# Moving the top-k mask to GpSimd and building the attention weights from transposed scores

## The chip, the cores and the metric

The kernel runs on one core of a Trainium2 chip. The metric is the device time of one execution in microseconds. The core's engines run beside each other: TensorE (matrix products and transposes; PE in the profile, with PEld for its weight loads), VectorE (DVE), ScalarE (ACT), GpSimd (POOL), and SyncE (SP), which issues transfers here. Products land in PSUM, everything else is held in SBUF.

## The reference, cut to what matters

Attention with a top-32 mask in each row of scores, for 8 batches of 8 heads, 576 rows and 64 columns a head, then a mixture of experts over the 4608 tokens with a capacity of 80 per expert. The change concerns the first part alone.

```python
def _attn_ref(q, k, v):                       # (8, 8, 576, 64) each
    top_k = 32
    scale = 1.0 / np.sqrt(D)
    scores = scale * np.matmul(q, k.transpose(0, 1, 3, 2))
    kth = np.partition(scores, -top_k, axis=-1)[..., -top_k:-top_k + 1]
    mask = scores >= kth
    scores = np.where(mask, scores, -1000000000.0)
    scores = scores - np.max(scores, axis=-1, keepdims=True)
    attn = np.exp(scores)
    attn = attn / (np.sum(attn, axis=-1, keepdims=True) + 1e-09)
    return np.matmul(attn, v).astype(np.float32)

# then: x = attention output as (4608, 512); top-1 expert by x @ w_gate;
# each expert keeps its 80 tokens of largest gate weight;
# out = gate * relu(x @ w1[e]) @ w2[e] for those, 0 for the rest
```

## The kernel before

The work goes by head pairs: `n` counts 32 of them (8 batches, 4 pairs of heads). Each pair has four full blocks of 128 query rows and a tail block of 64. A full block gives two *units* (one per head), the tail one unit with both heads' 64 rows stacked in the 128 partitions. So there are 9 units a pair and 288 in all. One *step* of the schedule handles one unit on VectorE, while other engines are at earlier or later units.

Scores are made once for the search (`front`) and scaled by a tiny power of two when ScalarE copies them out:

```python
TINY = 2.0 ** -48
minus = ...                      # identity in bf16, times -1.0 / TINY

def front(self, n, t):           # t: row block, 0 to 4
    ps = self.four()             # the one score buffer "sp": four PSUM banks, shared
    for j in range(2):
        for h in range(2):
            ...
            nc.tensor.matmul(o, lhsT=qT[d, ...], rhs=kT[d, ...], start=True, stop=True)
    s = self.rows.tile([P, 2 * S], F32, name="s", ...)
    nc.scalar.activation(s[...], ps[...], Act.Copy, scale=TINY)
```

VectorE finds the threshold of each row: the best 8 of six sixths, the best 24 of those 48, a count of how many scores lie above the 24th, and the 24th to 32nd from the rest. Then it makes the mask:

```python
def parts(self, i):              # "G", six times a unit
    nc.vector.max(out=cand[:, j, :], in_=s[:, j * S // NG : (j + 1) * S // NG])     # L202

def search(self, i):             # letters a b c d e, then y, g, h, m
    # a, c, e: best 8 of cand (L213); b, d: those taken out (L221);
    # with e: ScalarE writes y = sign(w9[7] - s) and counts (L218)
    nc.vector.tensor_tensor(out=y, in0=s, in1=y, op=Alu.mult)                      # y, L223
    nc.vector.max(out=w9[:, 8:], in_=y)                                            # g, L225
    nc.vector.scalar_tensor_tensor(out=pick, ..., accum_out=self.thr[:, i:i+1])    # h, L228
    self.drop(i)                                                                   # m

def drop(self, i):                                                                 # L250
    self.mask[i] = self.rows.tile([P, S], BF16, name="mask", ...)
    nc.vector.tensor_scalar(self.mask[i], s, self.thr[:, i : i + 1], top[:, 0, 0:1],
                            op0=Alu.is_lt, op1=Alu.add)   # (s < threshold) + row maximum
```

The weights are needed with the keys in the partitions, so `turn_w` makes the scores a second time, transposed. The mask, transposed by a product with `minus`, is added first in the same PSUM sum. It brings both the masking and the subtraction of the row maximum; ScalarE then takes the exponential:

```python
def turn_w(self, n, t):
    for h in range(2):
        for c in range(NK):      # five groups of keys
            nc.tensor.matmul(dst[h][c], lhsT=masks[h][:, keys[c]], rhs=eye[h],
                             start=c in (0, NF), stop=False, ...)                  # L268
    for c in range(NK):
        for h in range(2):
            nc.tensor.matmul(dst[h][c], lhsT=kT[heads[h], keys[c]], rhs=qT[heads[h], rows],
                             start=False, stop=True, ...)                          # L272
    nc.scalar.activation(wT[...], ab[...], Act.Exp, scale=scale)                   # L275
    nc.scalar.activation(wT[:, 2 * NF, :m], cc[:, :m], Act.Exp, scale=scale)       # L276

def back(self, n, t):            # weights times (v, ones): sums and unnormalised output, L290
    ...
def norm(self, n, ...):          # z = 1 / sum (z, L301, L304); xn = xu * z on GpSimd (L307);
    ...                          # xn to DRAM; later its transposes through "sp" (L165), the copy
                                 # xT (L320), and the gate product lp (L325), 128 columns at a time
def turn(self, n):               # the pair's q and k transposed through "sp" (L165), copies qT, kT (L176)
    ...
```

One step issues, in this order (a letter's number is how many units it lags behind):

```python
back = dict(a=0, b=1, c=1, d=1, e=1, y=2, g=2, h=3, m=3)
for c in "GbGcGdGehGmyGga": ...
turn_w(unit i - 3)               # if it closes a row block
front(unit i + 2) or turn(next pair)
back(unit i - 4)
norm's next part
```

Of the kernel before, what the change touches and what calls it, by code (L numbers as in the profile page):

```python
# [19 lines left out]
LOW = -3.0e38  # L20
TINY = 2.0 ** -48
# [3 lines left out]
def kernel(  # L25
# [11 lines left out]
    nc = tc.nc  # L37
# [31 lines left out]
    zero = const.tile([P, Dm], F32, name="zero")  # L69
# [19 lines left out]
    nc.scalar.mul(minus, ident, -1.0 / TINY)  # L89
# [16 lines left out]
    def clear():  # L106

        r = 4 * P
        return [lambda i=i: nc.sync.dma_start(
            out[i : i + r, :].rearrange("(p r) d -> p r d", p=P),  # L110
            zero.unsqueeze(1).to_broadcast([P, r // P, Dm])) for i in range(0, N, r)]

    class Attention:


        def __init__(self, stack, lean):
            self.lean = lean
            pool = lambda name, bufs, **kw: stack.enter_context(tc.tile_pool(name=name, bufs=bufs, **kw))
            self.nat, self.qkp, self.rows = pool("nat", 1), pool("qkp", 2), pool("rows", 2)
            self.small, vpool = pool("small", 4), pool("vpool", 1)  # L120
            self.ps_s, self.ps_w, self.ps_c = (pool(n, k, space=PSUM) for n, k in (("ps_s", 1), ("ps_w", 1), ("ps_c", 2)))
            self.qk, self.turned, self.lg = {}, {}, {}
            self.s, self.top, self.low, self.cnt, self.y, self.mask, self.w, self.xu = ({} for _ in range(8))

            self.thr = vpool.tile([P, HP * UPP if lean else NU], F32, name="thr")

            self.vb = []
            for j in range(1 if lean else 3):
                t = vpool.tile([P, NF, 2, D + 1], F32, name=f"vb{j}")
                r = vpool.tile([P, 2, D + 1], F32, name=f"vr{j}")  # L130
                nc.gpsimd.memset(t[:, :, :, D : D + 1], 1.0)
                nc.gpsimd.memset(r, 0.0)
                for h in range(2):
                    nc.gpsimd.memset(r[TL * h : TL * h + TL, h, D : D + 1], 1.0)
                self.vb.append((t, r))

            self.xT = vpool.tile([P, NK * P], F32, name="xT")
            nc.gpsimd.memset(self.xT[:, S:], 0.0)

        def load(self, n, b, hp):  # L140
            one = bass.ds(b, 1)
            tiles = []
            for name, src in (("qn", q), ("kn", k)):
                t = self.nat.tile([P, NK, 2, D], F32, name=name, tag=name)
                for h in range(2):
                    nc.sync.dma_start(
                        t[:, 0:NF, h, :],
                        src[one, 2 * hp + h, : NF * P, :].rearrange("o (c p) d -> p (o c) d", p=P))
                nc.sync.dma_start(
                    t[0:TL, NF, :, :], src[one, 2 * hp : 2 * hp + 2, NF * P :, :].rearrange("o h p d -> p (o h) d"))  # L150
                tiles.append(t)
            t, r = self.vb[n % len(self.vb)]
            for h in range(2):
                nc.sync.dma_start(
                    t[:, :, h, :D], v[one, 2 * hp + h, : NF * P, :].rearrange("o (c p) d -> p (o c) d", p=P))
                nc.sync.dma_start(r[TL * h : TL * h + TL, h, :D], v[one, 2 * hp + h, NF * P :, :].rearrange("o p d -> p (o d)"))
            self.qk[n] = tiles
# [10 lines left out]
        def turn(self, n):  # L168

            ts_ = []  # L170
            four = self.four()
            for j, (src, name) in enumerate(zip(self.qk.pop(n), ("qT", "kT"))):
                t = self.qkp.tile([P, S], F32, name=name, tag=name)
                ps = four[:, 2 * j : 2 * j + 2, :].rearrange("p j c -> p (j c)")
                self.turn_in(ps, src.rearrange("p c h d -> p c (h d)"))
                nc.scalar.copy(t, ps[:, :S])  # L176
                ts_.append(t)
            self.turned[n] = ts_
# [18 lines left out]
        def parts(self, i):  # L197

            s = self.s[i]
            cand = self.small.tile([P, NG, 8], F32, name="cand", tag="cand")  # L200
            for j in range(NG):
                nc.vector.max(out=cand[:, j, :], in_=s[:, j * S // NG : (j + 1) * S // NG])  # L202
                yield
            self.top[i] = cand.rearrange("p j c -> p (j c)")

        def search(self, i):
# [24 lines left out]
            self.drop(i)  # L231
            yield
# [13 lines left out]
        def drop(self, i):  # L246

            s, top = self.s.pop(i), self.top.pop(i)
            self.mask[i] = self.rows.tile([P, S], BF16, name="mask", tag="mask", bufs=3)
            nc.vector.tensor_scalar(self.mask[i], s, self.thr[:, i : i + 1], top[:, 0, 0:1], op0=Alu.is_lt, op1=Alu.add)  # L250

        def turn_w(self, n, t):

            qT, kT = self.turned[n]
            i = n * UPP + 2 * t
            m = P if t < NF else TL
            masks = [self.mask.pop(i), self.mask.pop(i + 1)] if t < NF else [self.mask.pop(i)] * 2
            eye = [minus, minus] if t < NF else [minus[:, :TL], minus[:, TL:]]
            ab = self.ps_w.tile([P, 2, NF, P], F32, name="ab", tag="ab")
            cc = self.ps_c.tile([P, 512], F32, name="cc", tag="cc")  # L260
            rows = slice(t * P, t * P + m)
            keys = [slice(c * P, min(c * P + P, S)) for c in range(NK)]
            heads = [slice(D * h, D * h + D) for h in range(2)]
            dst = [[ab[:, h, c, :m] for c in range(NF)] + [cc[heads[h], :m]] for h in range(2)]

            for h in range(2):
                for c in range(NK):
                    nc.tensor.matmul(dst[h][c], lhsT=masks[h][:, keys[c]], rhs=eye[h], start=c in (0, NF), stop=False,  # L268
                                     skip_group_check=True)
            for c in range(NK):  # L270
                for h in range(2):
                    nc.tensor.matmul(dst[h][c], lhsT=kT[heads[h], keys[c]], rhs=qT[heads[h], rows], start=False, stop=True,  # L272
                                     skip_group_check=True)
            wT = self.rows.tile([P, 2 * NF + 1, P], F32, name="wT", tag="wT")
            nc.scalar.activation(wT[:, : 2 * NF, :m], ab.rearrange("p h c r -> p (h c) r")[:, :, :m], Act.Exp, scale=scale)  # L275
            nc.scalar.activation(wT[:, 2 * NF, :m], cc[:, :m], Act.Exp, scale=scale)  # L276
            self.w[n, t] = wT, cc

        def back(self, n, t):
# [4 lines left out]
            vb, vr = self.vb[n % len(self.vb)]  # L284
            m = P if t < NF else TL
            for h in range(2):
                o = slice(P + h * (D + 1), P + (h + 1) * (D + 1))
                for c in range(NK):
                    for r in range(0, m, TL):
                        nc.tensor.matmul(cc[r : r + TL, o], lhsT=wT[:, h * NF + c if c < NF else 2 * NF, r : r + TL],  # L290
                                         rhs=vb[:, c, h, :] if c < NF else vr[:, h, :], start=(c == 0), stop=(c == NF))
            nc.scalar.copy(self.xu[n][:m, t, :, :].rearrange("p h d -> p (h d)"), cc[:m, P : P + 2 * (D + 1)])  # L292

        def norm(self, n, b, hp, bi, nb):
# [4 lines left out]
            z = self.small.tile([P, NK, 2], F32, name="z", tag="z")  # L299
# [15 lines left out]
            while self.fronts:  # L315
                yield
            ps = self.four()[:, :2, :].rearrange("p j c -> p (j c)")
            self.turn_in(ps, xn)
            xT = self.xT
            nc.scalar.copy(xT[:, :S], ps[:, :S])  # L320
            yield
            ps = self.ps_c.tile([P, 512], F32, name="lp", tag="cc")
            lp = ps[:, : NK * E].rearrange("p (c e) -> p c e", e=E)
            for c in range(NK):
                nc.tensor.matmul(lp[:, c, :], lhsT=xT[:, c * P : (c + 1) * P], rhs=wg[:, hp, :], start=True, stop=True)  # L325
# [5 lines left out]
            else:  # L331
                part = self.small.tile([P, NK, E], F32, name="part", tag="part", bufs=2)
# [38 lines left out]
        def run(self, slow):  # L371
# [10 lines left out]
            def step(i):  # L382
# [10 lines left out]
                back = dict(a=0, b=1, c=1, d=1, e=1, y=2, g=2, h=3, m=3)  # L393
                for c in "GbGcGdGehGmyGga":
# [3 lines left out]
                    elif c == "a":  # L398
                        if i < NU:
                            next(first[i], None)  # L400
                            second[i] = self.search(i)
                            next(second[i])
                    elif i - back[c] in second:
                        next(second[i - back[c]])
                j = i - 3
# [7 lines left out]
                j = i - 4  # L413
# [10 lines left out]
            with tc.manual_schedule():  # L424
# [6 lines left out]
                while i < NU + 4 or later:  # L431
# [4 lines left out]
        def judge(self):  # L436

            small = self.small
            least = small.tile([P, 1], F32, name="least", bufs=1)
            nc.vector.tensor_reduce(least, self.thr, axis=AX, op=Alu.min)  # L440
            ps = self.ps_c.tile([P, 512], F32, name="tp", tag="cc")
            nc.tensor.transpose(ps[:1, :P], least, ident)
# [265 lines left out]
```

## Time and profile before

| | before |
|---|---|
| device time, median of 3 | 1344.43 us (1344.4 to 1352.03) |
| span of the profiled execution | 1341.7 us |
| VectorE busy | 1127.2 us (84%) |
| TensorE busy | 1081.9 us (81%) |
| ScalarE busy | 679.1 us (51%) |
| GpSimd busy | 91.8 us (7%) |
| mean granted TensorE clock | 0.908 of full |

Busy times are unions over each engine's instructions; TensorE's are pipelined, so its share is an upper view of its work. In the lines of the profile, "L202" is a line of the kernel before. A group's line gives the engine, the operation, output<-inputs, the count, then busy time in us, mean ns of one, and the idle time of the engine just before these instructions with what ended it. A line of the waits gives the engine and line that waited, for whom, then the sum in us, how many times, and the longest.

### The profile page before, as it was taken

The page shows a single profiled execution, that of the slowest core. Times are in us where ns is not written, and L with a number is a line of the kernel's source. Part 1 is how long each engine was busy: PE and PEld are TensorE (multiplying, and loading weights), DVE is VectorE, ACT ScalarE, POOL GpSimd, SP SyncE. Part 2 cuts the span into 40 slices and gives each one's busy share as a digit, 9 for nine tenths or more (in the row PEclk, how much of TensorE's full clock was granted, in tenths as well). Part 3 has the DMA queues.
Part 4 walks back from the last instruction along what each step waited for, and adds up shares of the span by engine and source line. Part 5 has one row for each costly group of instructions (what it writes and reads, how often), then busy time and mean ns, then how long its engine had stood idle before and what let it go on. Part 6 is the DMA issues. An engine that isn't in the chain of part 4 may idle for free.

```text
span 1341.7 us, 38270 instructions
## 1 busy us (share of the span) xinstructions
PE 1081.9 (81%) x14862; PEld 834.7 (62%) x14862; DVE 1127.2 (84%) x5383; ACT 679.1 (51%) x1374; POOL 91.8 (7%) x213
## 2 busy tenths in 40 slices
PE   6888888888888888888888888888888888713987
PEld 3666666666666666666666666666666666603887
DVE  5999989999998999999999998999999999585001
ACT  4565555566555556565565556555555565300111
POOL 0000000000000000000000000000000000100111
PEclk9998989999889899898899989898898998855899
DMA  5033322222222122222222211111110110120660
GB/s 142 7 96 100 99 84 69 68 68 69 68 68 56 49 63 64 60 60 59 68 68 69 53 37 37 37 37 33 33 36 21 28 37 11 30 114 5 214 221 24
DMA packets 154590, 85.93 MB, mean 64 GB/s; under 512 B 118304, under 2 KB 136736, under 8 KB 154400
## 3 DMA queue, kind: packets, MB, share of 16 engines
q1 hardware_dynamic: 153376, 80.78, 21.0%
q0 software_dynamic: 1024, 2.62, 0.7%
q8 instruction: 118, 1.93, 0.6%
q14 instruction: 72, 0.59, 0.2%
HBM read 63.19 MB, written 20.19 MB: 62 GB/s over the span
## 4 chain that ended last, share of the span: by engine, by line
PE 47%; DVE 41%; ACT 8%; issue 2%; POOL 0%; DMA 0%; POOLq 0%; DVEq 0%; ACTq 0%
PE sp L190 11%; DVE cand L202 10%; PE ab L272 9%; DVE mask L250 8%; PE cc L290 7%; DVE y L223 6%; DVE w L225 6%; DVE cand L221 4%; PE ab L268 4%; ACT s L195 4%; PE yp L616 3%; PE cc L272 3%; DVE top L213 2%; PE cc L268 2%; PE sp L165 2%
## 5 line engine op out<-in xcount | busy, mean ns | idle before, releaser
L202 DVE MAX8 cand<-s 128x8 f32<-128x96 f32 x1728 | 432.0, 250 | 76.2 <-ACT s L195 76.2
L190 PE MATMUL sp<-kT,qT 64*128 64x288 f32 (+1 forms) x1280 | 233.0, 490 | 48.3 <-ACT s L195 25.7
L275 ACT ACTIVATE wT<-ab 128x1024 f32<-128x1024 f32 (+1 forms) x160 | 150.1, 938 | 236.6 <-PE ab L272 236.6
L290 PEld LDWEIGHTS cc<-vb,wT 128*64 128x64 f32 x4608 | 197.7, 153 | 62.2 <-issue 47.2
L218 ACT ACTIVATE y<-s,w 128x576 f32<-128x576 f32 x288 | 222.9, 774 | 20.2 <-DVE w L213 19.9
L290 PE MATMUL cc<-vb,wT 128*64 128x65 f32 x4608 | 227.2, 241 | 0.0
L195 ACT ACTIVATE s<-sp 128x1152 f32<-128x1152 f32 (+1 forms) x160 | 165.5, 1034 | 112.3 <-PE sp L190 108.0
L223 DVE TENSOR_TENSOR y<-s,y 128x576 f32<-128x576 f32 x288 | 216.6, 752 | 3.4 <-ACT y L218 1.4
L225 DVE MAX8 w<-y 128x8 f32<-128x576 f32 x288 | 214.0, 743 | 0.1
L268 PEld LDWEIGHTS <-mask 128*128 128x128 bf16 (+1 forms) x1600 | 106.2, 101 | 168.2 <-DVE mask L250 122.1
L268 PE MATMUL ab<-minus,mask 128*128 128x128 bf16 (+1 forms) x1280 | 120.1, 216 | 110.0 <-DVE mask L250 106.9
L272 PE MATMUL ab<-qT,kT 64*128 64x128 f32 (+1 forms) x2560 | 193.3, 293 | 0.0
L190 PEld LDWEIGHTS sp<-kT,qT 64*128 64x128 f32 (+1 forms) x1280 | 122.3, 204 | 106.1 <-ACT s L195 44.4
L272 PEld LDWEIGHTS ab<-qT,kT 64*128 64x128 f32 x2560 | 163.6, 196 | 10.0
L250 DVE TENSOR_SCALAR mask<-s,thr,top 128x576 bf16<-128x576 f32 x288 | 166.8, 579 | 1.5 <-DVE cand L202 0.6
L213 DVE MAX8 top<-cand 128x8 f32<-128x48 f32 x576 | 111.3, 193 | 0.1
L221 DVE MATCH_REPLACE8 cand<-top,cand 128x48 f32<-128x48 f32 x576 | 111.3, 193 | 0.0
L290 PE MATMUL cc<-vr,wT 128*64 128x65 f32 x1152 | 97.5, 235 | 0.0
L268 PE MATMUL cc<-minus,mask 128*64 128x128 bf16 (+1 forms) x320 | 76.3, 238 | 0.0
L292 ACT COPY xu<-cc 128x130 f32<-128x130 f32 (+1 forms) x160 | 42.2, 264 | 64.7 <-PE cc L290 64.7
L290 PEld LDWEIGHTS cc<-vr,wT 128*64 128x64 f32 x1152 | 70.4, 151 | 0.0
L272 PE MATMUL cc<-qT,kT 64*64 64x128 f32 (+1 forms) x640 | 69.6, 297 | 0.0
(165 smaller groups left out, 996.1 us busy)
## 6 DMA issues: line engine op xcount, KB each, us to landing
w<-in_moe_w_dram SPq DMA_DIRECT2D x32, 512.0 KB, 4.7
w<-in_moe_w_dram SPq DMA_DIRECT2D x8, 2048.0 KB, 12.9
out_dram<-zero SPq DMA_DIRECT2D x9, 1024.0 KB, 8.2
qn<-in_q_dram SPq DMA_DIRECT2D x64, 128.0 KB, 2.7
kn<-in_k_dram SPq DMA_DIRECT2D x64, 128.0 KB, 2.7
vb<-in_v_dram SPq DMA_DIRECT2D x64, 128.0 KB, 2.4
xd<-xn SPq DMA_DIRECT2D x32, 256.0 KB, 2.4
qn<-in_q_dram SPq DMA_DIRECT2D x32, 32.0 KB, 2.8
```

The costliest lines, as they stand in the source:

```text
L190: nc.tensor.matmul(o, lhsT=qT[d, t * P : t * P + m], rhs=kT[d, j * HS : (j + 1) * HS], start=True, stop=True)
L195: nc.scalar.activation(s[:, : g * S].rearrange("p (j c) -> p j c", c=HS), ps[:, : 2 * g, :HS], Act.Copy, scale=TINY)
L202: nc.vector.max(out=cand[:, j, :], in_=s[:, j * S // NG : (j + 1) * S // NG])
L218: nc.scalar.activation(y, s, Act.Sign, bias=w9[:, 7:8], scale=-1.0, accum_out=cnt)
L221: nc.vector.match_replace(out=cand, in_to_replace=dst, in_values=cand, imm_value=LOW)
L223: nc.vector.tensor_tensor(out=y, in0=s, in1=y, op=Alu.mult)
L225: nc.vector.max(out=w9[:, 8:], in_=y)
L250: nc.vector.tensor_scalar(self.mask[i], s, self.thr[:, i : i + 1], top[:, 0, 0:1], op0=Alu.is_lt, op1=Alu.add)
L268: nc.tensor.matmul(dst[h][c], lhsT=masks[h][:, keys[c]], rhs=eye[h], start=c in (0, NF), stop=False, skip_group_check=True)
L272: nc.tensor.matmul(dst[h][c], lhsT=kT[heads[h], keys[c]], rhs=qT[heads[h], rows], start=False, stop=True, skip_group_check=True)
L275: nc.scalar.activation(wT[:, : 2 * NF, :m], ab.rearrange("p h c r -> p (h c) r")[:, :, :m], Act.Exp, scale=scale)
L290: nc.tensor.matmul(cc[r : r + TL, o], lhsT=wT[:, h * NF + c if c < NF else 2 * NF, r : r + TL], rhs=vb[:, c, h, :] if c < NF else vr[:, h, ...
```

## The change

The mask is made on GpSimd, as a single comparison with the threshold (1 where the score is below it), and without the row maximum: the exponential is taken of unshifted scores. In `turn_w` the second score product is gone. The scores that the search already has in SBUF are transposed into PSUM, and the mask's product with `minus` (now minus the identity) is added to them: a masked score becomes about -1 where scores are scaled by 2^-48, and the exponential with scale/TINY sends it to zero. The tail block is transposed with both heads at once, so v's tail rows are laid out to match (`vb` holds all five key groups, and the last covers the last 128 keys, with zeros in v for the keys that the fourth group has already).

So that a sum of exponentials that became too small is noticed, the final test of thresholds (`judge`), which leads to a slower path, also looks at 1/sum (`z`). The schedule lags by one more unit, the order in a step is new, the transposes of xn use the small PSUM buffers instead of "sp", and q and k are both transposed before either is copied.

```diff
-            self.drop(i)
-            yield
+        def below(self, i):
+            self.top.pop(i)
+            self.mask[i] = self.rows.tile([P, S], BF16, name="mask", tag="mask", bufs=3)
+            nc.gpsimd.tensor_scalar(self.mask[i], self.s[i], self.thr[:, i : i + 1], None, op0=Alu.is_lt)
 ...
 turn_w:
-            for h in range(2):
+            for h in range(g):                      # g = 2, in the tail 1
+                sc = self.s.pop(i + h)
                 for c in range(NK):
-                    nc.tensor.matmul(dst[h][c], lhsT=masks[h][:, keys[c]], rhs=eye[h], start=c in (0, NF), stop=False,
-                                     skip_group_check=True)
-            for c in range(NK):
-                for h in range(2):
-                    nc.tensor.matmul(dst[h][c], lhsT=kT[heads[h], keys[c]], rhs=qT[heads[h], rows], start=False, stop=True,
-                                     skip_group_check=True)
+                    nc.tensor.matmul(dst[h][c], lhsT=sc[:, keys[c]], rhs=ident, start=c == 0 or (c == NF and h == 0), stop=False,
+                                     is_transpose=True, skip_group_check=True)
+            for h in range(g):
+                mk = self.mask.pop(i + h)
+                for c in range(NK):
+                    nc.tensor.matmul(dst[h][c], lhsT=mk[:, keys[c]], rhs=minus, start=False, stop=True, skip_group_check=True)
+            nc.scalar.activation(wT[...], ab[...], Act.Exp, scale=scale / TINY)
 ...
 turn: both sets of transposes, then both copies
 norm:
-            while self.fronts:
-                yield
-            ps = self.four()[:, :2, :].rearrange("p j c -> p (j c)")
-            self.turn_in(ps, xn)
+            ps, rest = (self.ps_c.tile([P, 512], F32, name="xp", tag="cc") for _ in range(2))
+            ...
-                nc.tensor.matmul(lp[:, c, :], lhsT=xT[:, c * P : (c + 1) * P], rhs=wg[:, hp, :], start=True, stop=True)
+                for r in range(0, P, TL):
+                    nc.tensor.matmul(lp[r : r + TL, c, :], lhsT=xT[:, c * P + r : c * P + r + TL], rhs=wg[:, hp, :],
+                                     start=True, stop=True)
 ...
 the step:
-                back = dict(a=0, b=1, c=1, d=1, e=1, y=2, g=2, h=3, m=3)
-                for c in "GbGcGdGehGmyGga":
+                back = dict(a=0, b=1, c=1, d=1, e=1, y=2, g=3, h=4, m=4)
+                for c in "GhmbGcGdGeGGgay":         # m is now self.below, on GpSimd
 ...
-                j = i - 3                           # turn_w
+                j = i - 4
-                j = i - 4                           # back
+                j = i - 5
 ...
 also: the zeros that clear the output are a 128x128 tile in place of 128x512; fewer buffers for two small tiles
```

## The prediction

> **What bounds the kernel now.** I read the busy shares first, then the two engines in order of time, then the waits. The page's first part and its slices:
>
> ```profile
> PE 1081.9 (81%) x14862; PEld 834.7 (62%) x14862; DVE 1127.2 (84%) x5383; ACT 679.1 (51%) x1374; POOL 91.8 (7%) x213
> ...
> PE   6888888888888888888888888888888888713987
> DVE  5999989999998999999999998999999999585001
> POOL 0000000000000000000000000000000000100111
> ```
>
> VectorE is at nine tenths in nearly every slice up to the 34th, TensorE at eight: the attention stage. The last seventh of the span (routing and experts, from about 1160 us) the change doesn't touch. Shares alone do not say which of two busy engines sets the pace, so I went to VectorE in order of time, one unit (128 query rows of one head) from one threshold to the next:
>
> ```profile
> 603.43 0.26 DVE L202 MAX8 cand<-s 128x8 f32<-128x96 f32 x1
> 603.62 0.58 DVE L250 TENSOR_SCALAR mask<-s,thr,top 128x576 bf16<-128x576 f32 x1
> 604.12 0.75 DVE L223 TENSOR_TENSOR y<-s,y 128x576 f32<-128x576 f32 x1
> 604.79 0.25 DVE L202 MAX8 cand<-s 128x8 f32<-128x96 f32 x1
> ...
> 607.07 0.26 DVE L202 MAX8 cand<-s 128x8 f32<-128x96 f32 x1
> 607.26 0.58 DVE L250 TENSOR_SCALAR mask<-s,thr,top 128x576 bf16<-128x576 f32 x1
> ```
>
> The columns are start, duration, then the instruction. There is no gap in it: the period is 607.26 - 603.62 = 3.64 us. There are 288 units, so 288 x 3.64 = 1048 us. The groups by line say where VectorE did stand still, and the waits what TensorE did meanwhile:
>
> ```profile
> L202 DVE MAX8 cand<-s 128x8 f32<-128x96 f32 x1728 | 432.0, 250 | 76.2 <-ACT s L195 76.2
> L250 DVE TENSOR_SCALAR mask<-s,thr,top 128x576 bf16<-128x576 f32 x288 | 166.8, 579 | 1.5 <-DVE cand L202 0.6
> ```
>
> ```profile
> PEld L268 <- DVE mask L250: 122.1, 91, 2.6
> ACT s L195 <- PE sp L190: 108.0, 129, 2.4
> PE ab L268 <- DVE mask L250: 106.9, 91, 2.4
> ```
>
> 1048 + 76 us of waiting for scores, and some 14 us of reciprocals and gating, make 1138 us, which is the stage: its first search instruction starts at 12.0, its last L202 at 1151.3. So VectorE is the bound. TensorE waits 107 us for masks. The 76 us are about two stops per head pair (57 in all), the longer ones near 1.9 us, where two score products for successive row blocks must pass through the one score buffer (sp) in PSUM.
>
> **What the Trainium skill says.** *GPSIMD Engine Reference*, section 4.1 Engine selection: elementwise work with two inputs is about twice as slow there as on VectorE, with one input roughly at line rate. The trace before has no wide one-input operation on that engine; its two-input product xn (128x512) takes 1043 ns and its 128x8 add 237 ns. *SBUF — State Buffer*, section Who interferes with whom: a VectorE instruction with two SBUF inputs and a GpSimd instruction that reads SBUF exclude each other for the whole instruction; one-input VectorE instructions outside the two-port modes don't. The trace before can neither show nor deny it: its y products (L223) all last 742 to 760 ns, but GpSimd is at 7%. *TensorE: Matmul & The Clock Gate*, section Part 1: the clock falls to half after a window without enough work. The trace agrees: between 20 and 1140 us the mean granted clock is 0.93, and in the stretch 626 to 630 us, after a 1.67 us wait for a mask, it is 0.50.
>
> **The change part by part.** *VectorE loses the mask.* The next instruction starts 604.12 - 603.62 = 0.50 us after it (the 579 ns overlap their neighbours). 288 x 0.50 = 144 us, all on the engine that sets the pace. The period becomes 3.14 us, and 288 x 3.14 = 904 us. Nothing else of the search changes, only its order.
>
> *GpSimd gains the mask.* 288 comparisons of 128x576, one input. Low estimate: this engine's fill of 128x640 takes 621 ns, or about 1 ns an element with its fixed part, so 237 + 568 x 0.85 = 0.72 us. High: the two-input rate from xn, (1043 - 388)/(512 - 128) = 1.7 ns an element, so 237 + 568 x 1.7 = 1.2 us. I take 0.9: 260 us in all, under a third of the stage, so the engine is not a bound. The mask is issued just after the threshold, near a step's beginning. The one wide two-input VectorE instruction, y, is now the step's last, 2.4 us after it by the row durations. So they should not meet, except where the xn product (1.4 us with its second part) stands in GpSimd's queue: once per head pair, up to 0.4 us. 32 x 0.4 = about 12 us back.
>
> *TensorE swaps score products for transposes.* From TensorE in order of time:
>
> ```profile
> 611.55 0.40 PE L268 MATMUL ab<-minus,mask 128*128 128x128 bf16 x4 [0.48 <-DVE mask L250]
> 611.87 0.24 PE L268 MATMUL cc<-minus,mask 128*64 128x128 bf16 x1
> 612.05 1.16 PE L272 MATMUL ab<-qT,kT 64*128 64x128 f32 x16
> 613.14 0.44 PE L272 MATMUL cc<-qT,kT 64*64 64x128 f32 x4
> 613.50 0.66 PE L165 MATMUL sp<-ident,xn 128*128 128x128 f32 x4
> ```
>
> The second score product takes 613.50 - 612.05 = 1.45 us (20 passes: each f32 product appears twice). Four f32 transposes last 0.66 us; less the 0.27 of the last one, 0.39/3 = 0.13 us from one to the next, so ten take 1.3 to 1.5 us. On a full row block the swap is even. The gain is elsewhere. The 64-row tail block, now with both heads in one set of rows, does five transposes and five mask products (0.7 + 0.5 = 1.2 us) for 2.04 us before (696.43 to 698.47). The gate product in halves costs about 20 x 0.03 (from L290's rate) instead of 10 x 0.11: 0.5 us less. All ten input transposes now come before their two copies, so about 1 us of waiting for the qT copy goes (27.2 us in the waits). Per head pair, full clock: before 4 x (1.0 masks + 1.45 + 1.17 scores + 1.32 weights times v) + 3.85 tail + 1.55 turn + 0.77 + 1.14 = 27.1 us; after about 25.8. VectorE's nine units take 9 x 3.14 = 28.3 us. TensorE fits, but with 9% to spare where it had 17% (27.1 of 32.8).
>
> *What is reordered.* Transposes need only scores, so they run while a mask is still being made: the 107 us wait for masks should mostly go, and with it many half-clock stretches. The xn transposes leave the score buffer (its 21.9 us wait for xT goes). Both shorten the chain that gave VectorE's 76 us of stops. I estimate 35 left, a gain of 41. One more step of pipeline adds 3 us at the end, the new test of z about 1 us.
>
> Sum: 1344.4 - 144 - 41 + 12 + 4 = 1175 us.
>
> **The rivals.** (a) VectorE stays the bound and its stops stay too: 1344.4 - 144 + 12 + 4 = 1216. For it: the single sp buffer remains, and TensorE's share rises. Against: two of its users' waits are removed. (b) TensorE becomes the bound. At 9% to spare, any half-clock stretch stops VectorE. If TensorE were productive only 80% of the time, 25.8/0.8 = 32.3 us a head pair, 32 x 32.3 = 1032 us instead of 1138: 1238. For it: the clock at half for 7 us about once per head pair before. Against: those stretches follow mask waits. (c) GpSimd is slower than estimated. Up to about 2 us nothing happens; beyond, y waits for the port and each further 0.1 us costs 29 us. A mask of 2.5 us would use up the gain and leave 1300 to 1350. Against: even the two-input rate gives 1.2 us. (d) No stops at all and no collisions: 1344.4 - 144 - 76 + 4 = 1128, the floor.
>
> **Range and chances.** Between the floor and (b), 1130 to 1245, I put eight chances in ten, the middle at 1175. Faster by over 2% means under 1317.5: only a bad case of (c), or (b) with much waiting, gets there. Faster 0.90, within 2% 0.04, slower 0.06.
>
> **What would show it.** Right: the search period 3.14 us, L202's idle time near 35 us, the mask on GpSimd at 0.7 to 1.2 us, y still about 750 ns, ten transposes in about 1.4 us, the granted clock in the stage above 0.95. Wrong: y's mean or L202's idle time grown (port or TensorE), a wait of TensorE for GpSimd's mask as large as the old one, or a mask over 2 us.

## The result and the profile after

The changed kernel takes 1174.45 us (median, 1173.9 to 1180.85) against 1345.61: a ratio of 0.873, 95% interval 0.869 to 0.877. The prediction was 1175. The sum held; four of the steps behind it did not, and the experiments below say which.

Page of the changed kernel, busy shares and slices:

```profile
PE 936.3 (80%) x13262; PEld 754.1 (64%) x13262; DVE 998.7 (85%) x5098; ACT 696.5 (59%) x1406; POOL 613.3 (52%) x496
...
PE   6888888888888888988888888888888887216997
DVE  6998998999999999899989998999899997682111
POOL 2565565665656665566656565556566666101101
```

The pattern is the old one with a shorter stage: VectorE at nine tenths, TensorE at eight. New is GpSimd at five to six tenths: its masks alone are busy for 497 us, about twice the 260 us planned.

The groups by line (the same search line is now L203, y L224, the mask L237):

```profile
L237 POOL TENSOR_SCALAR mask<-s,thr 128x576 bf16<-128x576 f32 x288 | 497.3, 1728 | 310.9 <-DVE cand L222 301.4
L203 DVE MAX8 cand<-s 128x8 f32<-128x96 f32 x1728 | 398.0, 244 | 48.1 <-ACT s L196 47.8
...
L224 DVE TENSOR_TENSOR y<-s,y 128x576 f32<-128x576 f32 x288 | 237.1, 823 | 0.0
```

The mask lasts 1728 ns, VectorE's stops for scores fell from 76 to 48 us, and y's mean rose from 752 to 823 ns. VectorE in order of time, y to y:

```profile
502.85 0.73 DVE L224 TENSOR_TENSOR y<-s,y 128x576 f32<-128x576 f32 x1
503.51 0.24 DVE L203 MAX8 cand<-s 128x8 f32<-128x96 f32 x1
...
505.97 1.08 DVE L224 TENSOR_TENSOR y<-s,y 128x576 f32<-128x576 f32 x1
```

The period is 505.97 - 502.85 = 3.12 us, as predicted (3.14). It is also the median over all 288 units. The second y lasts 1.08 us: a delayed GpSimd mask had begun at 505.70. The usual case is the xn product, in 30 of the 32 head pairs. GpSimd first, then VectorE, both in order of time:

```profile
520.46 1.72 POOL L237 TENSOR_SCALAR mask<-s,thr 128x576 bf16<-128x576 f32 x1 [1.51 <-DVE cand L222]
522.15 1.91 POOL L311 TENSOR_TENSOR xn<-xu,z 128x512 f32<-128x512 f32 x2
```

```profile
522.34 1.47 DVE L224 TENSOR_TENSOR y<-s,y 128x576 f32<-128x576 f32 x1
```

This y began 0.19 us after xn and took twice its usual 0.74 us. 288 x (0.823 - 0.739, its median) = 24 us in all. Most of it is xn: 30 x 0.73 = 22.

TensorE's waits:

```profile
PE ab L274 <- POOL mask L237: 106.8, 87, 2.3
ACT wT L276 <- PE ab L274: 104.0, 129, 3.1
```

The wait for masks is 106.8 us, where it was 106.9 for VectorE's mask. It did not go.

### The profile page after: what moved, and what is told of

Read it like the earlier page. It is cut to its first block, busy times and chain, and to the rows that moved or that the text cites. A ratio compares the mean times of both kernels' runs of the same rounds, so it can differ in the third digit from the quotient of the medians.

```text
span 1172.7 us, 35081 instructions
## 1 busy us (share of the span) xinstructions
PE 936.3 (80%) x13262; PEld 754.1 (64%) x13262; DVE 998.7 (85%) x5098; ACT 696.5 (59%) x1406; POOL 613.3 (52%) x496
## 4 chain that ended last, share of the span: by engine, by line
DVE 60%; PE 18%; ACT 7%; POOL 7%; issue 6%; DMA 0%; SPq 0%; POOLq 0%; ACTq 0%; DVEq 0%
DVE cand L203 17%; DVE y L224 13%; DVE w L226 11%; DVE cand L222 6%; POOL mask L237 6%; ACT s L196 4%; DVE top L214 4%; PE yp L629 3%; DVE pick L229 3%; PE sp L191 2%; ACT wT L276 2%; PE cc L294 2%; DVE w L214 2%; PE ab L274 2%; PE ab L269 2%
## 5 line engine op out<-in xcount | busy, mean ns | idle before, releaser
L237 POOL TENSOR_SCALAR mask<-s,thr 128x576 bf16<-128x576 f32 x288 | 497.3, 1728 | 310.9 <-DVE cand L222 301.4
L203 DVE MAX8 cand<-s 128x8 f32<-128x96 f32 x1728 | 398.0, 244 | 48.1 <-ACT s L196 47.8
L224 DVE TENSOR_TENSOR y<-s,y 128x576 f32<-128x576 f32 x288 | 237.1, 823 | 0.0
L274 PE MATMUL ab<-minus,mask 128*128 128x128 bf16 x1152 | 112.3, 226 | 106.8 <-POOL mask L237 106.8
L196 ACT ACTIVATE s<-sp 128x1152 f32<-128x1152 f32 (+1 forms) x160 | 165.4, 1034 | 32.7 <-PE sp L191 31.5
L269 PE MATMUL ab<-ident,s 128*128 128x128 f32 x1152 | 183.1, 289 | 1.1 <-ACT wT L276 1.1
L274 PEld LDWEIGHTS <-mask 128*128 128x128 bf16 x1440 | 98.3, 101 | 124.4 <-POOL mask L237 122.2
L269 PEld LDWEIGHTS ab<-ident,s 128*128 128x128 f32 x1152 | 132.9, 146 | 21.3 <-ACT wT L276 11.7
L269 PE MATMUL cc<-ident,s 128*128 128x128 f32 x288 | 80.9, 281 | 0.0
L274 PE MATMUL cc<-minus,mask 128*128 128x128 bf16 x288 | 65.1, 226 | 0.0
L229 DVE SCALAR_TENSOR_TENSOR pick<-past,cnt,w 128x9 f32<-128x9 f32 x288 | 61.0, 212 | 0.0
L311 POOL TENSOR_TENSOR xn<-xu,z 128x512 f32<-128x512 f32 x64 | 60.5, 966 | 0.1
```

Of the source, the lines that this page charges most:

```text
L196: nc.scalar.activation(s[:, : g * S].rearrange("p (j c) -> p j c", c=HS), ps[:, : 2 * g, :HS], Act.Copy, scale=TINY)
L237: nc.gpsimd.tensor_scalar(self.mask[i], self.s[i], self.thr[:, i : i + 1], None, op0=Alu.is_lt)
L269: nc.tensor.matmul(dst[h][c], lhsT=sc[:, keys[c]], rhs=ident, start=c == 0 or (c == NF and h == 0), stop=False, is_transpose=True, skip_gr ...
L274: nc.tensor.matmul(dst[h][c], lhsT=mk[:, keys[c]], rhs=minus, start=False, stop=True, skip_group_check=True)
```

## The experiments

All were timed beside the kernel before on the same chip; its medians there were 1342 to 1350 us. Executions that ran over 1.5% above the fastest of their kernel, at a lower granted clock (one of second_product, two each of old_order_first and masks_late), are left out of the medians here. "Stops" are VectorE's idle time before its first search instruction, waiting for scores.

### mask_on_vector: the comparison back on VectorE

```diff
-            nc.gpsimd.tensor_scalar(self.mask[i], self.s[i], self.thr[:, i : i + 1], None, op0=Alu.is_lt)
+            nc.vector.tensor_scalar(self.mask[i], self.s[i], self.thr[:, i : i + 1], None, op0=Alu.is_lt)
```

> The changed kernel with the one comparison back on VectorE, all else as changed. My theory (VectorE sets the pace, the gain is the 0.50 us a unit that the mask took there): 288 x 0.50 = 144 us come back, less the some 24 us that y loses to GpSimd in the changed kernel, so about 1295 us; y back at 740 ns. Rival (the gain came from TensorE, which no longer makes the second score product): 1175 to 1200.

Measured: 1302.42 us, ratio 0.965 (0.963 to 0.968). Groups by line:

```profile
L203 DVE MAX8 cand<-s 128x8 f32<-128x96 f32 x1728 | 400.8, 246 | 9.8 <-ACT s L196 9.7
...
L237 DVE TENSOR_SCALAR mask<-s,thr 128x576 bf16<-128x576 f32 x288 | 167.6, 582 | 31.5 <-DVE pick L229 0.9
```

Given the rest of the change, the move is worth 1302 - 1174 = 128 us. VectorE's busy time rises by 1136.4 - 998.7 = 138 us. It gains 38 us of stops (48 to 10) and loses 31.5 us as the mask now stands right behind the threshold it reads (0.11 us each). With a slower VectorE the stops are nearly gone: the other engines keep up with this pace.

### second_product and product_first: is it less work on TensorE, or its place?

The schedule, GpSimd mask and buffers of the changed kernel; the weights from a second score product, as before, with the mask's products first:

```diff
-    # ten transposes of s (is_transpose), then the mask's products
+    for h in range(2):
+        for c in range(NK):
+            nc.tensor.matmul(dst[h][c], lhsT=masks[h][:, keys[c]], rhs=eye[h], start=c in (0, NF), stop=False, ...)
+    for c in range(NK):
+        for h in range(2):
+            nc.tensor.matmul(dst[h][c], lhsT=kT[heads[h], keys[c]], rhs=qT[heads[h], rows], start=False, stop=True, ...)
```

> The changed kernel's schedule, GpSimd mask and buffers, but with the mask product first and then the second score product from q and k as before (tail block and v layout as before too). My theory: TensorE's work per head pair rises by less than 1 us, to some 26.6 of VectorE's 28.1, and its mask waits can no longer be filled with transposes: 1185 to 1225. Rival (TensorE's relief is the gain): 1300 or more.

Measured: 1300.34 us, ratio 0.961 (0.957 to 0.965). My theory missed by about 75 us. The stops, from its groups by line:

```profile
L205 DVE MAX8 cand<-s 128x8 f32<-128x96 f32 x1728 | 398.5, 244 | 153.8 <-ACT s L198 153.6
```

Taken alone this speaks for the rival: 154 us of stops where the transposes leave 48. But two things differ between the kernels, how much TensorE does and whether it can do it before the mask is there. So the two loops were swapped (scores first with start, the mask's products after them with stop), the amount staying as it is:

> As second_product (schedule, GpSimd mask and buffers of the changed kernel, second score product), but with the score products first and the mask's products after them in the PSUM sum. The amount of TensorE work is that of second_product, only the place of the wait for the mask differs. If the order is what counts (work that needs no mask fills the wait): 1180 to 1220 us. If the amount counts (2.44 us for masks and second product on a full block against 1.80 us for transposes and masks): 1280 to 1305.

Measured: 1168.43 us, ratio 0.869 (0.864 to 0.874), not to be told from the changed kernel, and 12 us under the range for the order. Its groups by line:

```profile
L205 DVE MAX8 cand<-s 128x8 f32<-128x96 f32 x1728 | 397.6, 244 | 33.6 <-ACT s L198 33.4
```

Only the order of two loops moved 132 us. Ahead of the mask's products the second score product costs no time that these runs show; behind them, each wait for a mask is followed by 1.46 us more (503.13 to 504.59) before the next scores (sp) can begin. From second_product, TensorE in order of time:

```profile
503.13 1.16 PE L281 MATMUL ab<-qT,kT 64*128 64x128 f32 x16
504.23 0.44 PE L281 MATMUL cc<-qT,kT 64*64 64x128 f32 x4
504.59 1.24 PE L193 MATMUL sp<-kT,qT 64*128 64x288 f32 x8
```

TensorE's waits for masks, first in second_product, then in product_first:

```profile
PE ab L277 <- POOL mask L239: 129.0, 93, 2.1
PE ab L281 <- POOL mask L239: 46.6, 60, 1.9
```

So the swap shortens the wait itself as well as what follows it, and the granted clock between 20 and 970 us rises from 0.91 to 0.97 with it; no run tells these three apart. That the change does without a second product brought no time by itself.

### before_first: the same swap in the kernel before

```diff
 turn_w of the kernel before: the loop over kT, qT first (start), the loop over masks second (stop); nothing else
```

> The kernel before, with one thing changed: in turn_w the second score product comes first and the mask's products after it. Mask on VectorE, old schedule, old buffers. VectorE's period stays 3.64 us, so only its 76 us of stops can go: if work ahead of the wait is what frees TensorE here too, L202's idle time falls to 15 to 45 us and the time to 1290 to 1325. If the stops come from the score buffer alone: 1340 to 1347.

Measured: 1289.11 us, ratio 0.960 (0.953 to 0.967). Groups by line:

```profile
L202 DVE MAX8 cand<-s 128x8 f32<-128x96 f32 x1728 | 431.9, 250 | 36.3 <-ACT s L195 36.3
```

As expected, and one microsecond beyond the range, VectorE's stops halve, and it still works on masks. A third of the change's gain (56 to 58 of 171 us) could be had by swapping two loops.

### mask_only and old_order_first: is the new schedule needed?

```diff
 kernel before, drop():
-            nc.vector.tensor_scalar(self.mask[i], s, self.thr[:, i : i + 1], top[:, 0, 0:1], op0=Alu.is_lt, op1=Alu.add)
+            nc.gpsimd.tensor_scalar(self.mask[i], s, self.thr[:, i : i + 1], None, op0=Alu.is_lt)
 old_order_first: the same, and turn_w's loops swapped as in before_first
```

> The kernel before with nothing changed but the mask: one comparison on GpSimd in place of VectorE's two operations (no row maximum is subtracted). Old order of a step, old lags. My theory: VectorE's period falls to 3.14 us, but the mask now arrives 1.7 us and more after its threshold in a schedule with no slack for it, and it is issued just ahead of y, so y and mask exclude each other: 1230 to 1300, with L202's idle time and TensorE's mask waits well above before. Rival (order and buffers matter little): about 1200. Rival (TensorE's relief is the gain): 1340 or more.

Measured: 1528.67 us, ratio 1.132 (1.129 to 1.135): slower than the kernel before, where my theory had it faster. The time lies in the second rival's range, but mask_on_vector and product_first speak against that rival. The waits did grow as the theory said, by far more than it allowed for:

```profile
DVE cand L202 <- ACT s L195: 245.4, 107, 8.9
PEld L268 <- POOL mask L250: 187.9, 89, 3.5
PE ab L268 <- POOL mask L250: 175.5, 81, 3.4
```

VectorE stops 245 us for scores, and y waits another 101 us for ScalarE's sign. The mask lasts 1995 ns on average here, against 1728: the 153 masks that start while a y runs have a median of 2.23 us, the other 135 one of 1.72.

> The kernel before with two things changed: the mask as one comparison on GpSimd, and the second score product ahead of the mask's products. Old order of a step, old lags, old buffers. Together with mask_only (1529 us) and product_first (1168 us) it tells what the new schedule is worth. If filling the wait is enough: 1170 to 1220. If the step's new order and the extra lag are needed for a mask that takes 1.72 us: 1300 to 1450.

Measured: 1365.17 us, ratio 1.017 (1.007 to 1.028). With the score products first, the old schedule (order, lags and buffers) leaves the GpSimd mask slower than VectorE's (1289); the new one makes 1168 of it. What the order of a step and the lag are worth apart was not tested.

### through_sp: the buffers of norm and turn undone

```diff
-            ps, rest = (self.ps_c.tile([P, 512], F32, name="xp", tag="cc") for _ in range(2))
+            while self.fronts:
+                yield
+            ps = self.four()[:, :2, :].rearrange("p j c -> p (j c)")   # sp again
 and in turn: q transposed, copied, then k transposed, copied
```

> The changed kernel, but xn is transposed through the score buffer sp again, when no scores are due, and q's copy stands before k's transposes again. My theory: VectorE's stops for scores go from 48 back towards 76 us: 1185 to 1205. Rival (these stops were the larger part of the gain): 1240 or more.

Measured: 1223.37 us, ratio 0.906 (0.903 to 0.908): 49 us of the gain come from these two parts, more than the 10 to 30 expected. The loss is not where I looked: L202's stops are 27.6 us, fewer than 48, but y now waits 62.8 us for ScalarE's sign (in the changed kernel: none). One such wait, ScalarE first, then VectorE:

```profile
502.48 0.64 ACT L178 COPY kT<-sp 128x576 f32<-128x576 f32 x1 [1.50 <-PE sp L169]
504.76 0.27 ACT L295 COPY xu<-cc 128x130 f32<-128x130 f32 x1 [1.64 <-PE cc L293]
504.92 0.78 ACT L218 ACTIVATE y<-s,w 128x576 f32<-128x576 f32 x1
```

```profile
505.82 0.76 DVE L223 TENSOR_TENSOR y<-s,y 128x576 f32<-128x576 f32 x1 [3.66 <-ACT y L218]
```

The sign stands on ScalarE behind k's copy, which waits for k's transposes, and behind the copy of the weights' products (xu), which waits too. TensorE has stood 0.73 us for q's copy just before, and its mean granted clock from 501 to 505 us is 0.57. In 21 of the 22 longer waits of y the same two copies come first, so in this trace the loss stands at q's copy ahead of k's transposes and not at xn. The two parts were not undone one at a time.

### half_mask and probe: the mask's size

half_mask compares only the first 288 columns and lets TensorE read those twice. It leaves out half of the comparisons, so its output is not the reference's; all other engines do the same instructions.

```diff
-            nc.gpsimd.tensor_scalar(self.mask[i], self.s[i], self.thr[:, i : i + 1], None, op0=Alu.is_lt)
+            nc.gpsimd.tensor_scalar(self.mask[i][:, : S // 2], self.s[i][:, : S // 2], self.thr[:, i : i + 1], None, op0=Alu.is_lt)
 and the mask's products read columns 0, 128, 0, 128 and 160 on
```

> The changed kernel, but GpSimd compares only the first 288 of the 576 columns and TensorE reads those twice in place of the others. It leaves out half of the mask's comparisons, so its output is not the reference's; instructions on all other engines are as many and as large as before. If the mask's 1.72 us cost time (y held up by the port, TensorE waiting for masks): y back at 740 ns, which gives 24 us, TensorE's mask wait under 40 us, and part of the 48 us of stops: 1105 to 1145. If the mask's length is hidden: 1165 to 1175.

Measured: 1102.57 us, ratio 0.821 (0.816 to 0.825). Groups by line:

```profile
L203 DVE MAX8 cand<-s 128x8 f32<-128x96 f32 x1728 | 396.6, 243 | 9.2 <-ACT s L196 9.2
L237 POOL TENSOR_SCALAR mask<-s,thr 128x288 bf16<-128x288 f32 x288 | 289.0, 1004 | 477.6 <-DVE cand L222 464.3
...
L224 DVE TENSOR_TENSOR y<-s,y 128x576 f32<-128x576 f32 x288 | 212.8, 739 | 0.0
```

So 0.72 us less in each mask is worth 72 us: 24 by y, 39 by stops, 9 not attributed. A shorter mask ends earlier, xn starts earlier, and y comes only as xn ends (0.90 us after its start). The time is just under the range; the wait for masks fell less than expected, to 60 us, and TensorE's mean clock between 20 and 900 us is 1.00 where it was 0.94. The mask's length was not hidden.

The probe is the changed kernel with 36 GpSimd instructions ahead of it, three of each form, such as:

```diff
+        for _ in range(3):
+            G.tensor_scalar(pf_[:, :W], ps_[:, :W], 0.25, None, op0=Alu.mult)
```

> The changed kernel with 36 GpSimd instructions ahead of it, three of each form, and three comparisons on VectorE, so longer by their sum; only the durations in the trace are of use. The disputed size is the mask's 1.72 us where 0.9 was estimated. If a comparison is what costs: multiplications and copies of 128x576 take under 1 us, all comparisons about 1.7 whatever the output. If the bf16 output costs: f32 outputs under 1 us. If the scalar read from memory costs: the constant form under 1 us. If every one-input tensor_scalar costs 3 ns an element: all about 1.7, half a tile about 0.9, and only plain copies shorter.

The instructions at one line of it (min/median/max ns), for the mask's form, the multiplication, the double tile, the copy and the two-input product:

```profile
L102 POOL TENSOR_SCALAR p_b<-p_s,p_t x3: 1713/1714/1736, 2.4 to 9.2; 128x576 bf16<-128x576 f32 x3
...
L108 POOL TENSOR_SCALAR p_f<-p_s x3: 1645/1652/1652, 23.4 to 28.6; 128x576 f32<-128x576 f32 x3
...
L114 POOL TENSOR_SCALAR p_b<-p_s,p_t x3: 3187/3187/3201, 30.2 to 37.8; 128x1152 bf16<-128x1152 f32 x3
...
L118 POOL COPY p_f<-p_s x3: 654/654/654, 33.4 to 41.0; 128x576 f32<-128x576 f32 x3
...
L120 POOL TENSOR_TENSOR p_f<-p_s x3: 1387/1388/1390, 42.2 to 46.2; 128x576 f32<-128x576 f32 x3
```

The last of the four explanations holds: every tensor_scalar of this size takes 1.64 to 1.72 us, whatever its operation, output type or scalar; (3187 - 1714)/576 = 2.56 ns an element, half a tile 1.00 us. A copy takes 0.65. The whole run took 1205.37 us, with the added instructions.

### lg_late, masks_late, masks_late4: taking out the waits that are left

```diff
 lg_late:
                 nc.scalar.copy(part, lp)
+                yield
                 nc.gpsimd.tensor_tensor(out=lg, in0=lg, in1=part, op=Alu.add)
```

> The changed kernel, with the small GpSimd sum of gate parts (lg) issued one step later, so that it no longer stands in GpSimd's queue waiting 74 us in all for ScalarE's copy, with masks behind it. If late masks cost time: y's mean falls from 823 towards 770 ns and the time to 1150 to 1168. If not: 1172 to 1176.

Measured: 1170.15 us, ratio 0.871 (0.865 to 0.876), between the two ranges and no difference from the changed kernel. The queue's wait for ScalarE fell from 74 to 15 us, y's mean only to 815 ns: the 22 us by xn are still there, and only the 2 to 3 us by late masks went.

```diff
 masks_late: turn_w ends after the transposes; a step later, ahead of everything else:
+                j = i - 5
+                if 0 <= j < NU and units[j][2]:
+                    self.mask_w(*units[j][:2])      # the mask's products and the exponentials
 masks_late4: the same, mask bufs 3 -> 4, v tiles 3 -> 2
```

> The changed kernel, with the transposes where they are, but the mask's products (and the exponentials) one step later, so that TensorE finds every mask ready. GpSimd's masks and their meeting with y stay. If TensorE's 107 us wait for masks is what leads to VectorE's stops (through the late next score product and the half clock): the wait goes to nearly 0, L203's idle time from 48 to about 15, clock in the stage near 1.0: 1135 to 1155 us. If the exponentials' 1.4 us now stand openly between masks and back in every second block and take the wait's place: 1165 to 1190.

> As masks_late, with four mask buffers in place of three (and two of the v tiles in place of three, to make room). If GpSimd waits for TensorE to free a mask in masks_late, this is some us faster; if not, the same within 5 us.

Measured: 1321.42 us (ratio 0.983, 0.978 to 0.988) and 1321.83 us (0.984, 0.978 to 0.990). In the second the next pair's v is loaded over a v tile before its last products have read it, so its output is not the reference's; its work is the same. A fourth mask buffer brings nothing. The waits of masks_late4:

```profile
PE cc L301 <- ACT wT L284: 160.6, 124, 3.9
ACT s L196 <- PE sp L191: 126.0, 67, 3.7
...
DVE cand L203 <- ACT s L196: 114.1, 74, 9.6
```

The wait for masks is off the list's head, and TensorE waits 161 us for exponentials instead (13 in the changed kernel). The rival was right, and it cost more than it allowed for.

## Why the prediction was right

The kernels that tell the parts apart, in us:

| mask on | schedule and buffers | mask's products first | work without mask first |
|---|---|---|---|
| VectorE | old | 1345 (before) | 1289 |
| GpSimd | old | 1529 | 1365 |
| GpSimd | new | 1300 | 1168 (1174 by transposes) |
| VectorE | new | not run | 1302 (by transposes) |

*VectorE loses the mask: right.* 0.50 us a unit was predicted, 3.64 - 3.12 = 0.52 measured, 150 us. But the table qualifies it: the move gives 128 us only with the other two parts (1302 to 1174); move and new schedule together, without the other order on TensorE, give 45 to 50 (1300 against 1345, and against 1350 beside it); with the old schedule the move loses. The pace of a step is VectorE's only if every other engine keeps up.

*GpSimd's 0.9 us: wrong.* It is 1.73, above the high estimate of 1.2. The step that failed is taking a fill (621 ns for 128x640) as the rate of one-input arithmetic. The sentence that I drew on from the Trainium skill (*GPSIMD Engine Reference*, section 4.1 Engine selection: one input roughly at line rate) fits the copy here (654 ns) but not tensor_scalar (1714 ns), which is slower than the two-input product of the same size (1388 ns) and three times VectorE's 579. The measurement decides. The rival (c), that nothing happens up to about 2 us, was wrong too: half_mask shows 72 us between 1.73 and 1.00.

*y meets xn once a head pair: right in kind, half in size.* 0.4 us a pair was predicted, 12 us in all; it is 0.73 us in 30 pairs, and with some delayed masks 24 us. The exclusion that the Trainium skill states (*SBUF — State Buffer*, section Who interferes with whom) shows: y, with two inputs, goes from 0.74 to as much as 1.48 us beside a GpSimd instruction. The one-input search instructions keep their times. But that it lasts for the whole instruction does not fit the mask. From the changed kernel, GpSimd, then VectorE:

```profile
304.64 1.73 POOL L237 TENSOR_SCALAR mask<-s,thr 128x576 bf16<-128x576 f32 x1
```

```profile
305.74 0.74 DVE L224 TENSOR_TENSOR y<-s,y 128x576 f32<-128x576 f32 x1
```

This y begins 1.10 us into a mask that runs on for 0.63 us, and keeps its time. So do all 12 that begin so late in a mask. The eight that begin 0.26 to 0.40 us into one end 1.35 us after the mask's start, which is 0.61 + 0.74: a mask keeps y out for some 0.6 of its 1.72 us. The measurement decides.

*The swap on TensorE is even: wrong, and without effect.* TensorE in order of time, one full block:

```profile
515.81 0.66 PE L269 MATMUL ab<-ident,s 128*128 128x128 f32 x4
...
516.96 0.39 PE L274 MATMUL ab<-minus,mask 128*128 128x128 bf16 x4
...
517.24 0.39 PE L274 MATMUL ab<-minus,mask 128*128 128x128 bf16 x4
...
517.61 1.19 PE L191 MATMUL sp<-kT,qT 64*64 64x288 f32 x8
```

Ten transposes take 1.15 us (1.3 to 1.5 predicted) and ten mask products 517.61 - 516.96 = 0.65 (1.0 before). That is 1.80 against 2.45 us, 2.6 us less per head pair than I had reckoned. product_first does without this saving and is as fast.

*The wait for masks goes, the clock rises: wrong, and the mask's length is part of why.* The 107 us stayed, and the clock between 20 and 980 us is 0.94, not above 0.95. What running ahead gave is not a shorter wait but a shorter path after it: stops fell to 48 us, 28 gained of the 41 predicted. half_mask, with masks of 1.0 us, near the 0.9 that I had estimated, has stops of 9 us and a clock of 1.00, but still a wait of 60 us. product_first, with masks as long as here, waits 47 us and takes the same time as the changed kernel: the sum of the waits for masks does not tell the time.

So the sum was right partly by offsets, and that it came within 1 us is luck: two of the three signs named for being wrong appeared, y's mean grown (752 to 823 ns) and a wait for GpSimd's mask as large as the old one. Between the first and the last L203 the stage lasts 971.0 us, 168 less than before: 150 by the period, 28 by stops, -24 by y, which leaves 14. VectorE's busy time in these stretches, before and after:

```profile
12.00:1151.30 1139.30, 1060.00 (x5248) 0.93 0.21 56
12.40:983.40 971.00, 930.32 (x4959) 0.94 0.24 66
```

It stood still for 79.3 us and now for 40.7, 39 less. So some 10 of the 14 us are other waits that went, most of them before the gating (6.8 to 0.6) and before y (3.4 to 0); 4 are not attributed. The prediction had no term for them: its 1048 + 76 + 14 us met the stage because the 76 hold 8.8 us of waiting ahead of the first search instruction, outside the stage. Predicted were 144, 41 and -12. A longer mask cost more at y and in stops than planned; the period and these other waits gave it back.

## What to carry to other kernels

Where one accumulation takes some inputs early and one late, issue the products of the early inputs first and let the late one close the sum: here the swap of two loops was worth 58 us in the old kernel and 132 in the new, while the smaller amount of work by transposes (1.80 against 2.45 us a block) showed no gain. An operation moved to another engine must be given a place in the schedule there: the same move with the old order was 13% slower than not moving. Before planning a slot of a given length, time that very form of instruction on that engine.

## What the runs showed of the hardware that was not expected

- GpSimd: tensor_scalar 128x576 1.64 to 1.72 us for comparison, subtraction and multiplication, f32 or bf16; copy 0.65 us; two-input product 1.39 us.
- A GpSimd mask kept a two-input VectorE instruction out for about 0.6 of its own 1.72 us; the 128x512 product xn for about 0.92 of its 1.04 us (0.19 + 1.47 - 0.74).
- The small second part of xn (64x128) lasts 388 ns in the kernel before and averages 874 ns in the changed one: 903 to 908 in the 30 cases that start while y runs, 387 and 388 in the two others.
- Five bf16 mask products on a block take 0.28 us (516.96 to 517.24) when all five weight loads are 128 columns wide; with a fifth of 64 columns they took 0.50 us (611.55 to 612.05). The rows differ in this, but it was not tested alone.
